# The outputs' products of a recurrence, with the two halves of the heads in two column groups of the array

## The chip, the core and the metric

The kernel runs on one core of one Trainium2 chip. The metric is the device time of one execution in microseconds (us); lower is better. Three runs of the kernel before gave a median of 1437.52 us (1435.84 to 1438.68).

## What is computed

Three stages follow each other: a recurrence over 768 tokens for 4 x 8 heads, a mixture of eight experts with two experts for each token, and a dense feed-forward layer. Only the first matters for the change:

```python
state = np.zeros((B, H, D, D))                       # B, H, S, D = 4, 8, 768, 40
for t in range(S):
    y[:, :, t] = np.einsum('bhd,bhde->bhe', rt, state)
    Sa = np.einsum('bhde,bhe->bhd', state, at)
    state = state * wt[:, :, None, :] - np.einsum('bhd,bhe->bhde', Sa, bt) + np.einsum('bhd,bhe->bhde', vt, kt)
...
x = y.transpose(0, 2, 1, 3).reshape(B * S, H * D)    # 3072 tokens x 320, goes to the experts
```

## The kernel before, in words

**The recurrence by chunks.** The tokens are cut into 24 chunks of 32. The 32 heads form two sets of 16, and each chunk is worked through once for each set, so there are 48 steps (`chain`, L604). A set's 16 heads are two halves `sg` of 8. What belongs to a chunk and not to the state (decays, products within the chunk, a triangular solve) is made ahead of the steps by three generators, `prepare`, `solve` and `apply`, whose instructions are dealt out between the parts of a step by `pump` at due times counted in steps.

**One step.** TensorE's order in step g is: the new states (`s_mm`, L559, tile `cu`); the transposes of the states (`tr`, L576, tile `ct`); the vectors u of the next step (`u_mm`, L546, tile `cu`); the outputs of the step before (`y_mm`, L522, tile `Y`); the products of r with v (`rv_mm`, L591, tile `ct`). Between them `fill` puts the work of the generators and of the routing. VectorE multiplies the new states by their decay (L564) and masks the products with v into the tile `RR` (L602); `tr` of the next step uses the buffers of `ct` that L602 frees.

**The outputs.** `y_mm` makes 16 products in each step, one for each head: weights `RR` of 128 rows x 32 columns (32 tokens), a moving operand `KB` of 128 rows x 40. In the trace each product is two instructions, as all of these f32 products are, so a step has 32 on L522. The four steps of two chunks fill the 128 partitions of two tiles `Y0` and `Y1` (one for each half), 32 partitions for each step: step c writes partitions 32 (c mod 4) onward of both. All 16 products of a step thus use one column group of the array, at `tile_position=(0, 32 (c % 4))`. `u_mm`, `s_mm` and `rv_mm` have a loop over `sg` inside the loop over heads, and the two halves go to different column groups (96 and 32 in `u_mm`, 0 and 64 in `s_mm` and `rv_mm`). After the fourth step ScalarE copies the two tiles to SBUF and GpSimd multiplies them by the decays `EN` of the same 128 tokens (VectorE does both from step 33 on, L532). The rows are then stored for the experts (L1687).

**The decays EN.** `turns` (L294) makes a chunk's decays with tokens on partitions: the 64 rows of chunk i go to rows 64 (i mod 2) onward of a tile `EN` that two chunks share (L317). `load_et` (L257) moves a chunk's 64 rows from `EN` to the two halves of a tile `ET` with two DMAs on SyncE's queue (SP), and GpSimd multiplies them with `a` (L268).

**Queues.** TensorE, ScalarE, VectorE and GpSimd run in the order in which the program is written. All loads and stores of the steps are issued by SP, whose order is left to the framework's scheduler (L1705 names the four others alone). For each chunk it issues, among others: `ET` (L262, two DMAs), `v` (L500, twice), `r` (L511 twice, L505), `w` and `k`, `b` (L201), the store of the chunk's products for the solve (L288), the load of `KB` (L495), the store `knd` of k and b turned (L308), the solved factors `Tbd` (L385, four) and `a` (L254).

**The order of tokens.** `ORDER` (L780) lists, for each tile of 128 tokens, which tokens lie on its partitions. The routing noise is laid out by it on the host, and the result is stored by it in runs of 32 rows (L1646). Tile 2 (c // 4) + sg holds the half `sg`.

Of the kernel before, what the change touches and what calls it, by code (L numbers as in the profile page):

```python
# [11 lines left out]
F32 = mybir.dt.float32  # L12
# [8 lines left out]
B, H, S, D = 4, 8, 768, 40  # L21
# [5 lines left out]
NG = NP * NC  # L27
# [37 lines left out]
class Rec:  # L65


    def __init__(self, ctx, nc, tc, ins, emit_x, ident, share, late):
        self.share, self.late = share, late
        self.nc, self.tc, self.ins, self.emit_x = nc, tc, ins, emit_x  # L70
        P = lambda n, b, **k: ctx.enter_context(tc.tile_pool(name=n, bufs=b, **k))
        self.one = P("rone", 1)
        self.p2, self.px = P("r2", 2), P("rx", 3)
        self.pet = P("ret", 1)
        self.pen = P("ren", 6)
        self.ptm, self.pwe = P("rtm", 2), P("rwe", 14)
        self.pp, self.py = P("rpp", 2, space=PS), P("rpy", 1, space=PS)
        self.cu, self.ct = P("rcu", 2, space=PS), P("rct", 2, space=PS)
        self.pd = P("rd", 2, space=bass.MemoryType.DRAM)
        self.pkn = P("rkn", 16, space=bass.MemoryType.DRAM)  # L80
        self.ident = ident
        self.scaled, self.lscr, self.tscr, self.Ec = {}, {}, {}, {}
        self.at = {}
        self.KN, self.ZT, self.EN, self.WE = {}, {}, {}, {}
        self.Y = {}
        self.seq = range(NC)
        self.extra, self.later, self.fresh = [], [], 0

# [168 lines left out]
    def load_et(self, i):  # L257

        en, et = self.EN[i // 2], self.at[i][1]
        r = 64 * (i % 2)  # L260
        for ab in range(2):
            self.nc.sync.dma_start(out=et[64 * ab:64 * ab + 64], in_=en[r:r + 64, ab])  # L262

    def scale_a(self, i):
        self.ready = i + 1
# [28 lines left out]
    def turns(self, i):  # L294

        nc = self.nc
        pt4 = lambda: self.pp.tile([128, 512], F32, name="pp")
        half = lambda x: x.rearrange("p (h x) -> p h x", x=64)[:, :, 0:D]
        kn, kb, Ec = self.p2.tile([128, HH, D], F32, name="kn"), self.kbt(i), self.Ec.pop(i)
        flip = lambda out, x: nc.tensor.transpose(out, x, self.ident[0:RW, 0:RW])  # L300
        for sg in range(2):
            yield
            pt = pt4()
            for p in range(4):
                flip(pt[:, p * 128:p * 128 + RW], kb[0:RW, sg * 4 + p].rearrange("p b s c -> p (b s c)"))
            nc.scalar.copy(out=kn[:, sg * 8:sg * 8 + 8], in_=half(pt))
        self.KN[i] = self.pkn.tile([64, 2 * HH * D], F32, name="knd")
        (nc.scalar if i < OPT['dk'] else nc.sync).dma_start(out=self.KN[i].rearrange("r (c x) -> c r x", c=2), in_=kn.rearrange("p h d -> p (h d)"))  # L308
        if i % 2 == 0:
            self.EN[i // 2] = self.pen.tile([128, 2, PR, D], F32, name="EN")  # L310
        en, r0 = self.EN[i // 2], 64 * (i % 2)
        for sg in range(2):
            yield
            pt = pt4()
            for p in range(4):
                flip(pt[0:64, p * 128:p * 128 + RW], Ec[0:RW, sg * 4 + p, :])
            nc.scalar.copy(out=en[r0:r0 + 64, :, sg * 4:sg * 4 + 4, :].rearrange("t b p d -> t p b d"),  # L317
                           in_=half(pt[0:64]).rearrange("t (p b) d -> t p b d", b=2))
# [191 lines left out]
            for ab in range(2):  # L510
                nc.sync.dma_start(out=self.rbd[i % 2][64 * ab:64 * ab + D, ab].rearrange("p a b c -> p (a b c)"), in_=ins["r"][i, ab])  # L511

    def y_mm(self, g, sg):
        nc = self.nc
        c = g
        r0 = 32 * (c % 4)
        if c % 4 == 0:
            self.Y[sg] = self.py.tile([128, 8, D], F32, name=f"Y{sg}")
        y = self.Y[sg]
        for h in range(8):  # L520
            hh = sg * 8 + h
            nc.tensor.matmul(y[r0:r0 + 32, h, :], lhsT=self.RR[c % 4][:, hh, :],  # L522
                             rhs=self.KB[(c // 2) % 2][:, c % 2, 1, hh, :], start=True, stop=True,
                             tile_position=(0, r0))
        if c % 4 == 3:
            x = self.px.tile([128, 8, D], F32, name="X") if g < NG - 1 else self.last_x[sg]
            en = self.EN[c // 4]
            dve = g in OPT['yd'] or g >= OPT['yv']
            if not dve:
                nc.scalar.copy(out=x, in_=y)  # L530
                y = x
            (nc.vector if dve else nc.gpsimd).tensor_tensor(  # L532
                out=x.rearrange("t (p b) d -> t p b d", b=2), in0=y.rearrange("t (p b) d -> t p b d", b=2),
                in1=en[:, :, sg * 4:sg * 4 + 4].rearrange("t b p d -> t p b d"), op=ALU.mult)
            self.extra.append(self.emit_x(2 * (c // 4) + sg, x))
# [68 lines left out]
    def chain(self, g, fill):  # L604
        if g == 0:
            self.u_mm(0)
        if g < NG - 2:
            if OPT['va']:
                self.load_v(g + 2)
            if g % NP == 0 and OPT['rb'] == 0:  # L610
                self.load_rbd(g // NP + 1)
            if g % NP and OPT['ra'] == 1 and g + 1 < NG:
                self.load_r(g // NP + 1)
            if g % NP and OPT['kb'] == 1 and g > 1:
                self.load_kb(g // NP + 1)
            self.s_mm(g)
        fill()
        trs = []
        for sg in range(2):
            trs.append(self.tr(g, sg))  # L620
            fill()
        if g + 1 < NG:
            self.u_mm(g + 1)
        fill()
        for sg in range(2):
            if g:
                self.y_mm(g - 1, sg)
        if g + 2 < NG:
            if not OPT['va']:
                self.load_v(g + 2)  # L630
            if g % NP == 0 and OPT['ra'] == 0:
                self.load_r(g // NP + 1)
            if g % NP == 0 and OPT['rb'] == 1:
                self.load_rbd(g // NP + 1)
            if g % NP == 0 and g and OPT['kb'] == 0:
                self.load_kb(g // NP + 1)
        fill()
        self.rv_mm(g, trs)
        fill()
# [49 lines left out]
    def run(self):  # L689
        nc = self.nc  # L690
        INF = 1e9
        self.consts_a()
        self.consts_b()
        gens = [self.prepare(), self.solve(), self.apply()]
        pos = []

        def pump(tau):
            while min(pos) <= tau:
                i = pos.index(min(pos))

                while i and self.wants[i]():
                    i = self.wants[i]() - 1
                pos[i] = next(gens[i], INF)

        tag = [None]

        def side(k=0):


            if self.extra and (not self.later or not self.fresh and (k == 5 if self.hurry else k % 3)):  # L710
                if next(self.extra[0], INF) is INF:
                    self.extra.pop(0)
                return
            if tag[0] == "act" and k:
                return
            two = True
            self.fresh = max(0, self.fresh - 1)
            while self.later:
                tag[0] = next(self.later[0], INF)
                if tag[0] is INF:  # L720
                    self.later.pop(0)
                elif tag[0] == "two" and two:
                    two = False
                else:
                    break

        self.made = self.ready = self.solved = 0
        self.wants = [None, lambda: 0, lambda: 0]
        self.begin()
        pos += [next(g) for g in gens]  # L730
        pump(-9)
        pump(-1)
        pump(OPT["t0"])
        f = np.cumsum((0,) + OPT["f"]) / sum(OPT["f"])
        for c in range(NG):
            self.hurry = c >= OPT["hurry"]
            slot = iter(enumerate(f[1:]))

            def fill():
                k, x = next(slot)  # L740
                pump(self.tau(c + x))
                side(k)

            self.chain(c, fill)
            if c == 2:
                self.tables()
            if c == NG - 2:
                self.late()
        for sg in range(2):
            self.y_mm(NG - 1, sg)  # L750
        while self.extra or self.later:
            side(1)
            side(0)
# [24 lines left out]


ORDER = np.arange(N).reshape(2, 2, NT // 2, 2, 32).transpose(2, 1, 3, 0, 4).reshape(NT, 128)  # L780


def xrow(n):
# [953 lines left out]
```

## Time and profile before

| | |
|---|---|
| median of three runs | 1437.52 us |
| the profiled execution | 1428.78 us |
| its span, first to last instruction | 1427.0 us |
| mean granted TensorE clock | 0.914 |
| TensorE matmuls, weight loads | 1193.8 us (84%), 1139.8 us (80%) |
| VectorE, ScalarE, GpSimd | 862.7 us (60%), 665.6 us (47%), 625.5 us (44%) |
| matmuls on L522 | 1536, from 135.1 to 600.0 us |

Shares are of the span. A matmul's duration runs from its start to its modelled end, and neighbours overlap, so what a block of matmuls costs is read from the start of one block to the start of the next. "Idle before" is the time in which the engine did nothing ahead of an instruction, with the one that ended it.

### The profile page before, as it was taken

The page shows a single profiled execution, that of the slowest core. Times are in us where ns is not written, and L with a number is a line of the kernel's source. Part 1 is how long each engine was busy: PE and PEld are TensorE (multiplying, and loading weights), DVE is VectorE, ACT ScalarE, POOL GpSimd, SP SyncE. Part 2 cuts the span into 40 slices and gives each one's busy share as a digit, 9 for nine tenths or more (in the row PEclk, how much of TensorE's full clock was granted, in tenths as well). Part 3 has the DMA queues.
Part 4 walks back from the last instruction along what each step waited for, and adds up shares of the span by engine and source line. Part 5 has one row for each costly group of instructions (what it writes and reads, how often), then busy time and mean ns, then how long its engine had stood idle before and what let it go on. Part 6 is the DMA issues. An engine that isn't in the chain of part 4 may idle for free. (4 is left out here: it accounts for less than half of the span.)

```text
span 1427.0 us, 33994 instructions
## 1 busy us (share of the span) xinstructions
PE 1193.8 (84%) x13902; PEld 1139.8 (80%) x13902; DVE 862.7 (60%) x1570; ACT 665.6 (47%) x1419; POOL 625.5 (44%) x556
## 2 busy tenths in 40 slices
PE   3425778878787886786999999998898999999998
PEld 2325767767677775775999998998888999999998
DVE  8474838657593833272877876775336665556653
ACT  3423545545444433431443443443236666676664
POOL 5553735546271624162334533443045554454431
PEclk9557989989889988897999999999998999999999
DMA  6644667666755754424345545644245111110000
GB/s 152 156 134 127 163 159 187 173 164 178 174 128 119 133 95 89 132 86 133 106 125 173 161 147 168 214 133 155 77 138 132 28 35 32 28 47 10 15 15 20
DMA packets 147309, 165.64 MB, mean 116 GB/s; under 512 B 70295, under 2 KB 118423, under 8 KB 147127
## 3 DMA queue, kind: packets, MB, share of 16 engines
q1 hardware_dynamic: 136438, 140.85, 37.6%
q0 software_dynamic: 10688, 22.32, 5.9%
q8 instruction: 120, 1.97, 0.6%
q14 instruction: 63, 0.51, 0.1%
HBM read 116.06 MB, written 43.12 MB: 112 GB/s over the span
## 5 line engine op out<-in xcount | busy, mean ns | idle before, releaser
L1609 POOL TENSOR_TENSOR gl<-fh,gh 128x1024 fp32r<-128x1024 f32 x46 | 131.0, 2878 | 106.2 <-ACT gh L1625 102.8
L1251 PE MATMUL ph<-xh,w1h 128*128 128x256 f32 (+1 forms) x576 | 162.1, 294 | 8.3 <-ACTq L1403 5.2
L1251 PE MATMUL ph<-xl,w1h 128*128 128x256 f32 (+1 forms) x576 | 161.8, 294 | 0.1
L1577 PE MATMUL fps<-fxh,ih 128*128 128x256 f32 x576 | 157.7, 288 | 2.2 <-DVE fh L1579 2.2
L1577 PE MATMUL fps<-fxl,ih 128*128 128x256 f32 x576 | 155.0, 283 | 0.1
L1608 DVE TENSOR_TENSOR fh<-fh,fp 128x1024 f32<-128x1024 f32 x48 | 95.0, 2015 | 61.4 <-ACT fp L1607 61.4
L1271 PE MATMUL py<-w2h,hl 128*128 128x320 f32 x400 | 125.7, 314 | 6.2 <-DVE hl L1105 6.1
L1271 PE MATMUL py<-w2h,hh 128*128 128x320 f32 x400 | 129.3, 323 | 1.0 <-ACT y L1282 0.8
L1271 PE MATMUL py<-w2l,hh 128*128 128x320 f32 x400 | 125.2, 313 | 2.5 <-DVE w2l L1107 1.5
L1105 DVE SCALAR_TENSOR_TENSOR hl<-ph,hh 128x512 fp32r<-128x512 f32 (+1 forms) x104 | 69.0, 665 | 95.1 <-ACT hh L1103 85.6
L1251 PEld LDWEIGHTS ph<-xh,w1h 128*128 128x128 f32 x576 | 113.3, 197 | 9.1 <-issue 5.7
L1639 PE MATMUL fpy<-oh,gl 128*128 128x320 f32 x384 | 114.6, 310 | 0.0
L1639 PE MATMUL fpy<-oh,gh 128*128 128x320 f32 x384 | 114.3, 310 | 0.0
L1639 PE MATMUL fpy<-ol,gh 128*128 128x320 f32 x384 | 113.9, 308 | 0.0
L1251 PEld LDWEIGHTS ph<-xl,w1h 128*128 128x128 f32 x576 | 113.3, 197 | 0.5 <-DVE xl L1107 0.5
L1579 DVE COPY fh<-fps 128x512 f32<-128x512 f32 x96 | 64.8, 689 | 80.7 <-ACT fp L1578 75.7
L1251 PE MATMUL ph<-xh,w1l 128*128 128x256 f32 (+1 forms) x384 | 112.7, 293 | 0.0
L1577 PEld LDWEIGHTS fps<-fxh,ih 128*128 128x128 f32 x576 | 110.2, 191 | 2.5 <-DVE fh L1579 2.4
L1577 PEld LDWEIGHTS fps<-fxl,ih 128*128 128x128 f32 x576 | 110.2, 191 | 0.6 <-DVE fxl L1107 0.5
L1577 PE MATMUL fps<-fxh,il 128*128 128x256 f32 x384 | 108.5, 282 | 0.0
L1103 ACT ACTIVATE hh<-ph 128x512 fp32r<-128x512 f32 (+1 forms) x104 | 59.6, 580 | 90.6 <-PE ph L1251 82.7
L602 DVE TENSOR_TENSOR RR<-ct,mrv 64x256 f32<-64x256 f32 x96 | 40.6, 423 | 91.3 <-PE ct L591 77.7
(276 smaller groups left out, 3352.6 us busy)
## 6 DMA issues: line engine op xcount, KB each, us to landing
KB<-knd SPq DMA_DIRECT2D x24, 640.0 KB
share<-in_w_dram SPq DMA_DIRECT2D x8, 1280.0 KB
wa<-in_wa_dram SPq DMA_DIRECT2D x22, 422.9 KB
kb<-in_kb_dram SPq DMA_DIRECT2D x20, 416.0 KB
share<-in_w_dram SPq DMA_DIRECT2D x8, 1024.0 KB
knd<-kn SPq DMA_DIRECT2D x24, 320.0 KB
yb<-y SPq DMA_DIRECT2D x22, 320.0 KB
ST<-in_vn_dram SPq DMA_DIRECT2D x48, 128.0 KB
```

The lines of the kernel that those rows point to most:

```text
L602: nc.vector.tensor_tensor(out=ro, in0=rvv, in1=self.mrv[r, None, :].to_broadcast([64, 8, C]), op=ALU.mult)
L1103: nc.scalar.activation(out=hi, in_=src, func=AF.Relu if relu else AF.Copy)
L1105: nc.vector.scalar_tensor_tensor(out=lo, in0=src, scalar=0.0, in1=hi.bitcast(F32), op0=ALU.max, op1=ALU.subtract)
L1251: nc.tensor.matmul(ph[:, m % c], lhsT=a, rhs=b, start=(q == 0), stop=(q == len(ops) - 1))
L1271: nc.tensor.matmul(py, lhsT=a[:, m, ts], rhs=b[:, m], start=(m == 0 and q == 0), stop=(m == FC - 1 and q == 2))
L1577: nc.tensor.matmul(ph[:, i], lhsT=a, rhs=b, start=(q == 0), stop=(q == len(ops) - 1))
L1579: nc.vector.tensor_copy(h[:, 2 * m2:2 * m2 + 2], ph)
L1608: mul = lambda s: nc.vector.tensor_tensor(out=h[:, s], in0=h[:, s], in1=p[:, s], op=ALU.mult)
L1609: low = lambda s: (nc.vector if last and s.start % 8 else nc.gpsimd).tensor_tensor(out=gl[:, s], in0=h[:, s], in1=gh[:, s].bitcast(F32), o ...
L1639: nc.tensor.matmul(py, lhsT=a[:, m, ts], rhs=w[:, m], start=(q == 0), stop=(q == len(ops) - 1))
```

## The change

The loop over `sg` moves inside the loop over heads, and the second half's tile `Y1` is filled from partition 64 on, modulo 128. The two products that follow each other then write partitions 64 apart. For the rows of `Y1` to meet their decays, `EN` holds the second half's columns with the two chunks' rows exchanged; a chunk's 64 rows of `EN` are no longer contiguous in partitions over both halves, and `load_et` issues four DMAs of half the bytes. The tokens of the odd tiles are turned by 64 in `ORDER`.

```diff
     def load_et(self, i):
         en, et = self.EN[i // 2], self.at[i][1]
-        r = 64 * (i % 2)
         for ab in range(2):
-            self.nc.sync.dma_start(out=et[64 * ab:64 * ab + 64], in_=en[r:r + 64, ab])
+            for sg in range(2):
+                r, p = self.enrow(i, sg), slice(4 * sg, 4 * sg + 4)
+                self.nc.sync.dma_start(out=et[64 * ab:64 * ab + 64, p], in_=en[r:r + 64, ab, p])
+
+    def enrow(self, i, sg):
+        return 64 * ((i + sg) % 2)
...
-        en, r0 = self.EN[i // 2], 64 * (i % 2)
+        en = self.EN[i // 2]
         for sg in range(2):
+            r0 = self.enrow(i, sg)
...
-    def y_mm(self, g, sg):
+    def y_mm(self, g):
         nc = self.nc
         c = g
-        r0 = 32 * (c % 4)
         if c % 4 == 0:
-            self.Y[sg] = self.py.tile([128, 8, D], F32, name=f"Y{sg}")
-        y = self.Y[sg]
+            self.Y = [self.py.tile([128, 8, D], F32, name=f"Y{sg}") for sg in range(2)]
         for h in range(8):
-            hh = sg * 8 + h
-            nc.tensor.matmul(y[r0:r0 + 32, h, :], lhsT=self.RR[c % 4][:, hh, :],
-                             rhs=self.KB[(c // 2) % 2][:, c % 2, 1, hh, :], start=True, stop=True,
-                             tile_position=(0, r0))
-        if c % 4 == 3:
+            for sg in range(2):
+                hh = sg * 8 + h
+                r0 = (32 * (c % 4) + 64 * sg) % 128
+                nc.tensor.matmul(self.Y[sg][r0:r0 + 32, h, :], lhsT=self.RR[c % 4][:, hh, :],
+                                 rhs=self.KB[(c // 2) % 2][:, c % 2, 1, hh, :], start=True, stop=True,
+                                 tile_position=(0, r0))
+        for sg in range(2 if c % 4 == 3 else 0):
+            y = self.Y[sg]
...
 ORDER = np.arange(N).reshape(2, 2, NT // 2, 2, 32).transpose(2, 1, 3, 0, 4).reshape(NT, 128)
+ORDER[1::2] = np.roll(ORDER[1::2], 64, axis=1)
```

The two places that call `y_mm` now call it once for a step instead of once for each half.

## Rows read from the trace of the kernel before

**Rows 1.** Busy time of each engine by stretch; then TensorE's clock, DMA share, GB/s

```profile
135.00:465.00 330.00, 261.97 (x5433) 238.12 (x5427) 214.52 (x312) 164.31 (x483) 165.11 (x110) 0.89 0.64 159
465.00:600.00 135.00, 104.22 (x1935) 93.99 (x1932) 60.17 (x136) 51.59 (x160) 49.69 (x74) 0.85 0.53 104
600.00:800.00 200.00, 173.50 (x1216) 169.06 (x1214) 128.91 (x351) 72.88 (x160) 80.70 (x93) 0.93 0.44 127
800.00:1427.00 627.00, 600.53 (x4487) 594.56 (x4486) 371.98 (x668) 331.07 (x512) 270.07 (x190) 0.98 0.29 86
```

**Rows 2.** TensorE's waits, 135 to 465 us: total us, times, longest

```profile
PE cu L559 <- DMA KB<-knd: 26.3, 9, 5.9
PE ct L576 <- DVE RR L602: 25.9, 13, 5.9
PE cu L546 <- DMA ST<-in_vn_dram: 10.6, 6, 4.6
```

**Rows 3.** TensorE's waits for L602, 465 to 600 us

```profile
PE ct L576 <- DVE RR L602: 4.8, 2, 2.7
```

**Rows 4.** VectorE's waits for TensorE's L591, 465 to 600 us

```profile
DVE RR L602 <- PE ct L591: 36.5, 12, 10.6
```

**Rows 5.** SP's queue in order of time: start, us, line, DMA

```profile
293.87 1.15 SPq L262 DMA_DIRECT2D ET<-EN  x2
...
298.85 0.64 SPq L495 DMA_DIRECT2D KB<-knd  x1
299.58 0.55 SPq L308 DMA_DIRECT2D knd<-kn  x1
...
310.25 0.39 SPq L254 DMA_DIRECT2D AT<-in_at_dram  x1
314.46 1.15 SPq L262 DMA_DIRECT2D ET<-EN  x2
```

**Rows 6.** SP's waits, 135 to 465 us

```profile
SPq L262 <- DMA knd<-kn: 26.2, 10, 3.8
...
SPq L495 <- PE pp L300: 9.9, 2, 5.2
```

**Rows 7.** Groups of TensorE's matmuls by line and shape, 135 to 600 us

```profile
L522 PE MATMUL Y<-KB,RR 128*32 128x40 f32 x1534 | 73.4, 214 | 3.3 <-issue 3.3
...
L546 PE MATMUL cu<-ST,Zt 128*32 128x40 f32 x1460 | 43.6, 218 | 27.3 <-DVE ST L564 13.2 <-DMA ST<-in_vn_dram 10.6 <-issue 2.5
```

**Rows 8.** TensorE in order of time, a step at 294 us

```profile
294.28 0.77 PE L546 MATMUL cu<-ST,Zt 128*32 128x40 f32 x32 [0.43 <-DMA ST<-in_vn_dram]
294.84 1.31 PE L522 MATMUL Y<-KB,RR 128*32 128x40 f32 x32
296.09 0.57 PE L300 MATMUL pp<-ident,kb 104*128 104x104 f32 x4
```

**Rows 9.** TensorE in order of time, a step at 421 us

```profile
420.93 1.28 PE L546 MATMUL cu<-ST,Zt 128*32 128x40 f32 x32
422.00 2.08 PE L522 MATMUL Y<-KB,RR 128*32 128x40 f32 x32
424.02 0.58 PE L300 MATMUL pp<-ident,kb 104*128 104x104 f32 x4
```

**Rows 10.** The stretches of rows 8 and rows 9, columns as in rows 1

```profile
294.00:296.40 2.40, 2.12 (x67) 2.10 (x68) 0.00 (x0) 2.10 (x7) 0.00 (x0) 1.00 0.43 94
420.30:423.60 3.30, 3.30 (x60) 3.15 (x60) 3.23 (x3) 2.48 (x8) 3.22 (x2) 0.50 0.20 35
```

**Rows 11.** VectorE in order of time, at 330 us

```profile
330.03 3.51 DVE L227 TENSOR_TENSOR_SCAN R<-wa,d1b 104x529 f32<-104x529 f32 x1
333.57 0.88 DVE L602 TENSOR_TENSOR RR<-ct,mrv 64x256 f32<-64x256 f32 x2
```

**Rows 12.** TensorE in order of time, what follows rows 11

```profile
334.04 0.66 PE L576 MATMUL ct<-ident,ST 128*128 128x128 f32 x4 [1.93 <-DVE RR L602]
```

**Rows 13.** All DMA issues of L262: ns min/median/max, first and last start

```profile
L262 SPq DMA_DIRECT2D ET<-EN x44: 224/584/1653, 35.9 to 466.4; - x44
```

More of the change, by code (lines that the diff above doesn't have):

```diff
@@ L84, in __init__ @@
         self.KN, self.ZT, self.EN, self.WE = {}, {}, {}, {}
-        self.Y = {}
         self.seq = range(NC)
@@ L624, in chain @@
         fill()
-        for sg in range(2):
-            if g:
-                self.y_mm(g - 1, sg)
+        if g:
+            self.y_mm(g - 1)
         if g + 2 < NG:
@@ L748, in run @@
                 self.late()
-        for sg in range(2):
-            self.y_mm(NG - 1, sg)
+        self.y_mm(NG - 1)
         while self.extra or self.later:
```

## The prediction

> **What bounds the kernel now.** I read the stretches first, then each stretch's waits, then the queues in order of time. The change touches the 48 steps, 135 to 600 us; what follows is TensorE's (173.50 busy of 200 us, then 600.53 of 627) [rows 1] and, as data, stays the same, so I take an earlier or later end of the steps to move the end of the kernel by as much.
>
> The steps fall into two parts. Up to about 465 us there are 32 steps, and TensorE is busy 262 of 330 us [rows 1]. What it waits for there is not its own: the load of `KB` 26.3 us, VectorE's L602 25.9 us, the load of `v` 10.6 us [rows 2]. From 465 us on there are 16 steps and 104 us of work in 135 us; the wait for L602 is down to 4.8 us [rows 3], and it is VectorE that waits for TensorE, 36.5 us in 12 of the 16 steps [rows 4]. So TensorE paces the second part and mostly not the first.
>
> The pace of the first part is seen on SP. The `ET` loads start at 293.87 and again at 314.46 us, 20.6 us apart, which is two steps [rows 5]. Before the second, SP does nothing from 310.64 us on, and the wait is for the store `knd` [rows 5, 6]: issued at 299.58 us, it has landed 14.9 us later. From the first `ET` to that store SP issues one DMA behind another for 5.7 us [rows 5]. 5.7 + 14.9 = 20.6 us: SP and the DMAs alone make a loop as long as two steps. It is not always the last: in two chunks SP waited for TensorE ahead of `KB`, 9.9 us [rows 6].
>
> **The part that gains.** L522 is 1534 of the records of 135 to 600 us [rows 7]. What a step's 32 cost is read from block to block: at 294 us L546 takes 0.56 us from its start to that of L522, L522 1.25 us to the start of what follows [rows 8]. At 421 us it is 1.07 against 2.02 us [rows 9]. The granted clock is 1.00 in the first stretch and 0.50 in the second, the two levels 2.4 and 1.2 GHz [rows 10]. L546 has the same 32 instructions with weights of 128 x 32 and a moving operand of 128 x 40 [rows 7]; it differs in that neighbours write to different column groups, as L522's will. I take its price: 1.25 - 0.56 = 0.69 us at the full clock, of which I keep 0.6 us for a step, since a block that another shape follows pays for that change before and after, and about 0.95 us at the half clock. Below that, a gain of zero is possible if the alternation is not what makes L546 fast; above, 0.69 us is the most.
>
> A rule of the Trainium skill speaks against it: by the page "TensorE: Matmul & The Clock Gate", section "Part 3: Packing small matmuls — row/col tiling", a weight load overlaps running matmuls only where the row groups differ; here all use all 128 rows. By that L522 would stay at 1.25 us; the row of L546 [rows 8], all 128 rows too, does not agree, and I go by it.
>
> In the second part 12 steps, in which VectorE waits [rows 4], give 12 x 0.6 = 7.2 us; some half clock there and a few steps late in the first part in which nothing but TensorE is late add about 1.8 us. That is **-9.0 us**. In the rest of the first part I give the saving nothing: where a load or L602 is late, TensorE only waits longer. At 330 us, for one, VectorE is still in a 3.51 us scan when the products are long done, L602 follows at 333.57 us, and `tr` has waited 1.93 us [rows 11, 12]. If every step passed its saving on, it would be 48 x 0.6 = 29 us; the waits of [rows 2] exclude most of that.
>
> **The part that costs.** `load_et` issues two more DMAs for a chunk. The 44 issues took 584 ns in the median, 224 at the least [rows 13]; a pair at 314.46 us took 1.15 us [rows 5]. Half the bytes in the same 64 rows: no row shows the half size, so between 2 x 0.22 = 0.45 and 1.2 us; I take 1.2, since the issue keeps SP for the rows and not for the bytes as far as a neighbour in [rows 5] tells (`KB`, by its shape with eight times the bytes of one `ET` load, takes 0.64 us). They stand at the start of the 5.7 us ahead of the next `KB` and `knd`, behind the wait for the old `knd`, and queued behind them on SP are `v`, `r`, `w`, `KB` and `knd` themselves; for `KB` and `v` TensorE waits [rows 2]. The first part holds 330 / 20.6 = 16 chunks. In ten the wait for `knd` stands right ahead of `ET` [rows 6]; take off two in which SP waits for TensorE later anyway, and 8 x 1.2 = **+9.6 us** remain. Bounds: nothing, if SP's idle time takes the issues up; 12 x 1.2 = 14.4 us if the loop holds in all but the late chunks.
>
> **What costs nothing.** The same products, copies and multiplications run. The copies of Y0 used to start after half of the 1.25 us block; now after all of a block half as long, so no later. `turns` writes other partitions of `EN` with the same copies. The order of tokens changes no size. The halved rows of `ET` add 128 packets to a chunk; the DMA share in the first part is 0.64 [rows 1], and GpSimd's L268, which waits for `ET`, feeds work two chunks later; were that cover gone, it would be part of the 1.2 us bound. Two more DMAs may also shift which earlier DMA a later one of SP's waits is for; the one that SP stands at is ahead of the first `ET` [rows 5, 6] and stays there, so I put the rest at nothing, with the 14.4 us as its upper bound too.
>
> **Sum.** -9.0 + 9.6 = +0.6 us on the profiled 1428.78 us, 1429.4. The median of the runs lies 8.7 us above that execution, so 1438 us as a median: no change that a measurement of this kernel can tell (about 0.2%, 2.9 us).
>
> **The rivals.**
> *SP has room* (chance 0.27). The issues of half the size are short, or the loads have slack before TensorE needs them, and the loop's length does not matter. For it: in the steps at 330 us VectorE and not a load is last [rows 11, 12]. Against it: the 26.3 and 10.6 us of [rows 2]. Then -9 us stand alone: 1428.5 us.
> *SP's loop decides: slower* (0.19). The place is between the landing of one `knd` and the issue of the next; the price 1.2 us for a chunk; from 7.5 chunks on it eats the gain of 9 us, and from ten on the kernel is slower beyond doubt. With 12 chunks, 14.4 us, and 7 us gained because the last steps find another wait (their 4.8 us for L602 grow [rows 3]): +7.4, 1445 us. For it: the exact 5.7 + 14.9 of [rows 5].
> *The products do not overlap* (0.06). The change then does not do what it says: L522 stays at 1.25 us a block, and only the DMAs show: +9.6, 1447 us. Against it is L546 [rows 8]; this is the skill page's rule at work.
> *TensorE paces more than the waits show* (0.06): half of the first part's steps pass on 0.6 us too, and SP has room: -9 - 9.6, 1419 us.
>
> **How the numbers follow.** My forecast has 0.42 and a range of its own of 1433 to 1443: a couple of chunks or steps more or less. Of it 0.26 falls within 0.2%, 0.07 below, 0.09 above. SP's room gives 0.25 to faster and 0.02 to the same, the deciding loop 0.17 to slower and 0.02 to the same, the last two 0.06 each to slower and faster. Faster 0.38, same 0.30, slower 0.32. The range from 1427 to 1448 holds all but the last rival and the outer halves of the first two, within 2 in 10.
>
> **What the profile of the changed kernel would show.** The block of L522 at 0.55 to 0.65 us at the full clock; unchanged, the first step is wrong. Four `ET` issues in about 2.3 us, and `ET` to `knd` near 6.9 us; if it is 5.7 to 6.2, the price was too high. `ET` to `ET` near 21.8 us and TensorE's waits for `KB` and `v` clearly above 26.3 and 10.6 us: the loop holds. If two chunks still take 20.6 us, SP had room. The stretch from the end of the `ET` loads to the end of L522 some 8 us shorter. The forecast is wrong if the store `knd` is no longer what SP waits for, or if the scheduler orders SP's queue anew.

## The result, and the profile after

The changed kernel takes 1450.45 us in the median of six runs (1443.52 to 1455.35), the kernel before 1436.19 us (1430.49 to 1438.68) beside it: a ratio of 1.0111 [1.0077, 1.0144], 14 us slower. The forecast was no change, 1438 us, with a range up to 1448. The profiled execution took 1453.06 us with a span of 1451.3 us, against 1428.78 and 1427.0 us.

First the products themselves. TensorE in order of time in two steps of the changed kernel (start and duration in us), and below the two stretches with the granted clock third from the end:

```profile
305.81 0.80 PE L553 MATMUL cu<-ST,Zt 128*32 128x40 f32 x32 [0.31 <-DMA ST<-in_vn_dram]
306.42 0.76 PE L528 MATMUL Y<-KB,RR 128*32 128x40 f32 x32
307.11 0.58 PE L304 MATMUL pp<-ident,kb 104*128 104x104 f32 x4
...
392.12 1.33 PE L528 MATMUL Y<-KB,RR 128*32 128x40 f32 x32
393.38 0.96 PE L304 MATMUL pp<-ident,kb 104*128 104x104 f32 x4
```

```profile
391.50:393.50 2.00, 2.00 (x60) 1.91 (x55) 0.00 (x0) 0.91 (x3) 0.00 (x0) 0.50 0.36 85
306.40:307.10 0.70, 0.70 (x44) 0.66 (x37) 0.00 (x0) 0.52 (x3) 0.00 (x0) 1.00 0.37 92
```

From the start of the block of outputs (L528) to the start of what follows it is 0.69 us at a granted clock of 1.00 (2.4 GHz) and 1.26 us at 0.50 (1.2 GHz), against 1.25 and 2.02 us [rows 8, 9]. The two column groups do what they were to do: 0.56 us less per step at the full clock and 0.76 us at half of it.

The time is lost elsewhere. Busy time by stretch in the changed kernel (columns as in rows 1), and TensorE's waits from 135 to 465 us:

```profile
135.00:465.00 330.00, 239.94 (x5212) 216.70 (x5210) 212.35 (x309) 155.98 (x460) 160.90 (x107) 0.85 0.60 152
465.00:600.00 135.00, 90.23 (x1815) 81.08 (x1814) 57.65 (x131) 49.58 (x150) 48.19 (x73) 0.82 0.55 98
```

```profile
PE cu L566 <- DMA KB<-knd: 39.8, 10, 7.1
PE ct L583 <- DVE RR L609: 31.9, 9, 6.1
PE pp L407 <- DMA Tbd<-tscr: 6.1, 3, 2.3
PE cu L553 <- DMA ST<-in_vn_dram: 5.4, 4, 2.5
```

TensorE gets through fewer matmuls in the same 330 us (5212 against 5433 [rows 1]; of its busy time, 239.94 against 261.97 us, a part is only the shorter products), and waits 39.8 us for `KB` where it waited 26.3 us [rows 2]. Who makes `KB` late is seen on SP's queue, two steps in order of time, with SP's longest wait and all of its `ET` issues (ns min/median/max):

```profile
305.24 2.43 SPq L262 DMA_DIRECT2D ET<-EN  x4
...
311.26 0.64 SPq L500 DMA_DIRECT2D KB<-knd  x1
312.05 0.58 SPq L312 DMA_DIRECT2D knd<-kn  x1
312.69 1.92 SPq L505 DMA_DIRECT2D ST<-in_vn_dram  x1
314.66 0.34 SPq L510 DMA_DIRECT2D RR<-in_rt_dram  x1
315.04 7.78 SPq L390 DMA_DIRECT2D Tbd<-tscr  x4
322.93 1.51 SPq L253 DMA_DIRECT2D AT<-in_at_dram  x1
326.99 2.42 SPq L262 DMA_DIRECT2D ET<-EN  x4
```

```profile
SPq L262 <- DMA knd<-kn: 35.2, 12, 5.3
```

```profile
L262 SPq DMA_DIRECT2D ET<-EN x88: 461/595/1600, 35.1 to 489.2; - x88
```

From the first `ET` to `knd` it is 6.8 us (5.7 before [rows 5]), from there to the next `ET` 14.9 us as before, together 21.75 us for two steps in place of 20.6. With half the bytes an `ET` issue still takes 595 ns in the median (584 before [rows 13]). How this adds up over the 24 chunks is read from the first and the last issue of `knd`, of which each chunk has one. The kernel before, then the changed one:

```profile
L308 SPq DMA_DIRECT2D knd<-kn x24: 524/553/1451, 34.5 to 445.2; - x24
```

```profile
L312 SPq DMA_DIRECT2D knd<-kn x24: 528/554/714, 34.4 to 464.7; - x24
```

410.7 us became 430.3 us: +19.6 us before the 24th `knd`. Behind it, over the last 18 steps, the two are equal although the products are shorter: the last products start at 600.0 and at 619.2 us, 154.8 and 154.5 us after the last `knd`. The remaining 5 us of the spans' difference come later: ahead of the group L1257 (L1251 before) TensorE was idle for 13.7 us against 8.3 us, in a stage that the change does not touch.

### The profile page after: what moved, and what is told of

Its sections match the earlier page's. It is cut to its first block, busy times and chain, and to the rows that moved or that the text cites. A ratio compares the mean times of both kernels' runs of the same rounds, so it can differ in the third digit from the quotient of the medians.

```text
span 1451.3 us, 34061 instructions
## 1 busy us (share of the span) xinstructions
PE 1173.7 (81%) x13902; PEld 1118.2 (77%) x13902; DVE 859.9 (59%) x1570; ACT 665.1 (46%) x1419; POOL 621.4 (43%) x556
## 5 line engine op out<-in xcount | busy, mean ns | idle before, releaser
L1257 PE MATMUL ph<-xh,w1h 128*128 128x256 f32 (+1 forms) x576 | 162.2, 294 | 13.7 <-issue 10.0
L1257 PE MATMUL ph<-xl,w1h 128*128 128x256 f32 (+1 forms) x576 | 161.3, 293 | 0.5 <-DVE xl L1113 0.4
L1257 PEld LDWEIGHTS ph<-xh,w1h 128*128 128x128 f32 x576 | 113.3, 197 | 14.5 <-issue 10.5
L1257 PEld LDWEIGHTS ph<-xl,w1h 128*128 128x128 f32 x576 | 113.2, 197 | 0.9 <-DVE xl L1113 0.9
L1257 PE MATMUL ph<-xh,w1l 128*128 128x256 f32 (+1 forms) x384 | 112.0, 292 | 0.0
L583 PE MATMUL ct<-ident,ST 128*128 128x128 f32 x384 | 71.9, 322 | 44.3 <-DVE RR L609 43.1
## 6 DMA issues: line engine op xcount, KB each, us to landing
wa<-in_wa_dram SPq DMA_DIRECT2D x22, 422.9 KB
```

What stands on the lines that cost most here:

```text
L583: nc.tensor.transpose(tr[:, p, :], ST[:, sg * 4 + p].rearrange("p b x -> p (b x)"), self.ident)
L1257: nc.tensor.matmul(ph[:, m % c], lhsT=a, rhs=b, start=(q == 0), stop=(q == len(ops) - 1))
```

## The experiments

Each group of kernels was timed beside the kernel before on one chip. The time is the difference of the two medians; the ratio, with its 95% interval, is that of the runs of both and can differ from it by some us (the changed kernel again: +24.1 us, but 0.0139 x 1409 = 19.6 us). "knd" is the time from the first to the last issue of `knd` in the one execution that was profiled, as read above, against the 410.7 us of the kernel before; two executions of one kernel agree within 1 us (430.3 and 431.1, 410.7 and 409.7, 406.6 and 406.2). All results first, then the groups; "four loads" and "groups" are the two halves of the change.

| kernel | time against before, us | ratio | knd, us |
|---|---|---|---|
| four loads of ET alone | +20.5 | 1.0142 [1.0104, 1.0180] | 427.9 |
| three loads alone | +10.9 | 1.0070 [1.0047, 1.0094] | 419.7 |
| groups alone | -0.7 | 0.9988 [0.9961, 1.0014] | 407.7 |
| the changed kernel again | +24.1 | 1.0139 [1.0099, 1.0179] | 431.1 |
| before, again (one execution) | | | 409.7 |
| changed, two loads on ACT | +10.5 | 1.0080 [1.0051, 1.0109] | 424.6 |
| before, one load on ACT | -2.1 | 0.9994 [0.9962, 1.0026] | 405.5 |
| groups, one load on ACT | -2.9 | 0.9981 [0.9951, 1.0012] | 412.6 |
| before, knd on ACT | +18.2 | 1.0150 [1.0113, 1.0187] | 432.5 |
| changed, knd on ACT | +50.1 | 1.0368 [1.0333, 1.0404] | 460.0 |
| groups, knd on ACT | +12.6 | 1.0102 [1.0065, 1.0139] | 435.1 |
| before, products twice | +10.4 | 1.0085 [1.0050, 1.0119] | 409.9 |
| before, kb and wa on POOL | -5.2 | 0.9958 [0.9934, 0.9981] | 406.6 |
| changed, kb and wa on POOL | -2.5 | 0.9986 [0.9963, 1.0008] | 409.2 |
| spare loads behind knd | +14.4 | 1.0122 [1.0092, 1.0152] | 420.4 |
| spare loads behind ET | +17.4 | 1.0130 [1.0103, 1.0156] | 429.2 |
| groups, kb and wa on POOL | -14.0 | 0.9917 [0.9888, 0.9946] | 401.7 |
| before, kb and wa on POOL, again | -7.6 | 0.9948 [0.9925, 0.9971] | 406.2 |

**The two halves of the change, each alone.** The first kernel has the products as before and each `ET` load cut in two; the second has the column groups and two `ET` loads, `EN` and the token order as before; the copy of the second tile exchanges its halves instead, as two instructions of 64 rows each (where VectorE does the work, its multiplication). These few instructions are added work that the changed kernel does not have.

```diff
-            self.nc.sync.dma_start(out=et[64 * ab:64 * ab + 64], in_=en[r:r + 64, ab])
+            for sg in range(2):
+                p = slice(4 * sg, 4 * sg + 4)
+                self.nc.sync.dma_start(out=et[64 * ab:64 * ab + 64, p], in_=en[r:r + 64, ab, p])
```

```diff
+            rows = [(slice(0, 128), slice(0, 128))] if not sg else [(slice(0, 64), slice(64, 128)), (slice(64, 128), slice(0, 64))]
...
-                nc.scalar.copy(out=x, in_=y)
+                for o, s in rows:
+                    nc.scalar.copy(out=x[o], in_=y[s])
```

> The kernel before with ET loaded in four DMAs of half the bytes, and nothing else of the change (products of the outputs in one column group, EN and the order of tokens as before). If SP's loop is the cause: slower by 16 to 24 us (at least what the changed kernel loses, 14 us, as the shorter products no longer give anything back), ET to ET near 21.3 us for two steps. If the column groups are the cause (TensorE less busy, its clock granted less often): within 3 us of before, clock near 0.914. If it is the exchanged rows of EN or the turned tokens: within 3 us of before.

> The two halves in two column groups as in the changed kernel, but ET in two DMAs, EN and the order of tokens as before; the second half's rows are put back in place when Y is copied out (six more copies of ScalarE and a few more products of VectorE in all). If SP's loop is the cause: faster than before by 2 to 9 us, ET to ET near 19.8 to 20.6 us. If the column groups are the cause: slower by about 14 us, clock near 0.90. If EN or the tokens: faster or the same.

> The kernel before with ET loaded in three DMAs (one whole, two halves). If SP's loop is the cause and each issue has its price: about half of what four loads cost, slower by 8 to 12 us. If the column groups, EN or the tokens are the cause: within 3 us of before.

> The changed kernel itself, on the chip of the three others, so that the four cases (one or two column groups, two or four loads) stand side by side. By every theory 1.1% slower than before, 1446 to 1455 us. If SP's loop is the cause it is a little faster than the kernel with four loads and one column group, by the 2 to 9 us that the shorter products give.

The loads alone cost all of it (+20.5 us), the groups alone nothing that shows, and one added load costs half of what two do. The changed kernel and the four loads alone stand within their intervals of each other, so the groups win nothing that shows on top of the loads either, and there without the added copies. Both misses of the 2 to 9 us expected of the groups are taken up further below. TensorE's granted clock is too little changed to be the loads' cost: 0.914 in the median of the runs of the four loads alone, 0.918 in the kernel before beside them, and 0.004 x 1409 us are 6 us at most. TensorE's waits for `KB` in the four loads alone are those of the changed kernel:

```profile
PE cu L561 <- DMA KB<-knd: 39.7, 11, 6.4
```

**Two loads, or one, on another queue.** In each kernel the named loads are issued by ACT:

```diff
-                self.nc.sync.dma_start(out=et[64 * ab:64 * ab + 64, p], in_=en[r:r + 64, ab, p])
+                (self.nc.scalar if sg else self.nc.sync).dma_start(out=et[64 * ab:64 * ab + 64, p], in_=en[r:r + 64, ab, p])
```

> The kernel before once more, unchanged, for its trace beside those of the other runs of this chip. Its profiled execution should lie near 1409 us, the median that the kernel before had beside the first four experiments. Of its stretches: if the loss of the four loads lies in SP's loop alone, its 13 periods of two steps between the ninth and the 22nd landing of knd take about 257 us, as in the two column groups alone (257.0), against 271 to 275 with four loads; if it lies elsewhere, the periods are as long as with four loads and the tail is shorter.

> The changed kernel with its four loads of ET kept, two of them (the second half of heads) issued by ACT's queue and two by SP's as before. Bytes, packets and the number of transfers are those of the changed kernel. If SP's time for the two added issues is the loss, it is won back: 0 to 5 us against the kernel before (ratio 1.000 to 1.004), the periods of two steps back at 19.8 us from 21.2. If it is the added transfers themselves (packets, the transfers' landing), +20 to +24 us stay (1.014 to 1.017). If ACT, held by the two issues and by their wait for a free ET, takes SP's place, something in between or worse, with ACT's copies of EN late.

> The kernel before with one of its two loads of ET issued by ACT's queue: one issue per chunk less on SP. If SP's loop still sets the pace at its present length, the line through three and four loads (+10.9 and +20.5 us for one and two more) goes on below: -8 to -11 us (ratio about 0.993), 19.1 us for a period of two steps instead of 19.8. If the loop is only just the bound and another engine's pace lies close under it, 0 to -4 us. If ACT is the one held, slower, by 2 to 10 us.

> The two column groups alone (as in the second experiment), with one of the two loads of ET issued by ACT's queue. If the column groups bought nothing because SP's loop set the pace, then with SP relieved they pay: 3 to 9 us faster than the same relief without the groups. If TensorE's saved 0.6 us a step is absorbed by other waits as well (DVE's RR, the chain of the steps), the two are within 2 us of each other.

The kernel before once more took 1425 us in its one execution and not the 1409 us expected; its trace has the stall told of at the end, and its `knd` time is that of before. With two loads on ACT half of the loss comes back (+10.5 us): in between, as the third case had it, but the wait that shows is SP's. Its waits from 135 to 465 us in the changed kernel with two loads on ACT:

```profile
SPq L390 <- DMA ET<-EN: 24.9, 10, 12.2
SPq L510 <- DMA ET<-EN: 14.9, 2, 7.6
```

SP now stands at `Tbd` and `RR` until an `ET` transfer has landed, though neither reads `ET`; with all of `ET` on SP (the kernel before, the changed one, the four loads alone) SP has no wait for `ET`. One `ET` issue less on SP, with and without the groups, brings 2 to 3 us, inside the intervals and not the 8 to 11 of a line that goes on. This does not show how close SP's loop is to the next bound, since here, too, SP gained waits for `ET` (25.0 us at `Tbd` and 22.2 us at `AT` without the groups).

**knd on ACT's queue.** From the ninth chunk on, the store that SP waits for is issued by ACT (`nc.scalar if i >= 8`), in the kernel before, the changed one, and the groups alone.

> The kernel before with the store of knd issued by ACT's queue from the ninth chunk on. In the kernel before, SP waits at the first load of ET until knd has landed (some 14 us after its issue), and the next knd is issued some 6 us after that landing: 14 + 6 are the 20 us of a period of two steps. If this ring of knd's landing and the issues behind it is the pace, taking knd out of SP's queue opens it: periods of 17 to 19 us and 10 to 35 us less in all, or as much as the next bound allows. If the pace is the transfers' own rate or the chain of the steps, and SP only follows, the periods stay at 19.8 us and the time within 4 us of before. If ACT's own wait for a free place for knd's transfer takes the place of SP's, the periods stay or grow, with ACT late at TRs.

> The changed kernel, four loads of ET on SP and all, with knd issued by ACT's queue from the ninth chunk on. If the four loads cost what they do because they lie between one landing of knd and the issue of the next, most of their price goes with the ring: within 5 us of the same edit in the kernel before. If an added issue costs its SP time wherever SP is, or the added transfers cost their own time, the changed kernel stays 15 to 22 us behind the same edit in the kernel before.

> The two column groups alone (two loads of ET on SP, rows put back by the copy), with knd issued by ACT's queue from the ninth chunk on. If the column groups bought nothing because SP's ring set the pace, they pay here: 4 to 9 us less than the same edit in the kernel before. If their 0.6 us a step is lost in the chain of the steps too, the two are within 3 us.

All three got slower, which only the last case of the first expectation had. The changed kernel lost 50 us, 32 us more than the same move cost the kernel before, beyond both cases expected; the groups came out 5.6 us below it, as expected if they pay, but the two intervals overlap. The wait was not opened but moved; SP's waits of the kernel before with `knd` on ACT, 135 to 465 us:

```profile
SPq L500 <- DMA knd<-kn: 44.5, 4, 14.8
SPq L201 <- DMA knd<-kn: 30.6, 4, 10.9
SPq L1687 <- DMA knd<-kn: 22.8, 2, 11.5
SPq L505 <- DMA knd<-kn: 22.4, 2, 11.5
```

Loads that have no use for `knd` wait for it, up to 14.8 us at a time. In the changed kernel's queue, shown above, the first `ET` is the eighth DMA behind `knd` (`ST`, `RR`, four `Tbd`, `AT`, then `ET`; the kernel before has the same order), and `ET` does not read `knd` either. My guess, not shown, is that DMAs share a few completion counters in turn; the runs show which DMA waits for which, not the counters.

**The products twice.** `for h in (*range(8), *range(8))` in the kernel before: 55 us more work for TensorE.

> The kernel before with every block of the outputs' products done twice over, with the same result: 1.15 us more of TensorE per step at full clock (32 more instructions of 36 ns), 55 us over 48 steps. If TensorE paces only the last 16 steps, as the prediction had it, the time grows by 1.15 us in about 12 of them and by a little in the rest: 12 to 20 us. If TensorE has room nearly everywhere, 0 to 6 us. If TensorE paces the first part too, and the column groups' gain was lost for another reason, 40 to 55 us.

A block of 64 took 2.39 us, from its start to the next:

```profile
294.58 2.46 PE L522 MATMUL Y<-KB,RR 128*32 128x40 f32 x64
296.97 0.58 PE L300 MATMUL pp<-ident,kb 104*128 104x104 f32 x4
```

The 24 chunks took 409.9 us, as without the extra work: up to the last `knd` TensorE has room for 1.15 us a step more. What the time grew by lies behind it: 10.4 us by the medians, 12 us by the ratio (7 to 17 us by its interval), at the lower end of what was expected if TensorE paces the last steps alone. The 18 steps from the last `knd` to the last products, with the products twice and then in the four loads alone, a trace without the stall told of at the end as well (columns as in rows 1):

```profile
443.90:600.50 156.60, 133.73 (x2776) 125.10 (x2775) 62.49 (x142) 61.06 (x187) 50.34 (x77) 0.92 0.61 114
```

```profile
462.20:597.10 134.90, 111.00 (x2168) 103.03 (x2168) 61.91 (x140) 60.22 (x186) 49.16 (x74) 0.92 0.64 119
```

In the six traces with one column group and without the stall this stretch takes 133 to 137 us, so the doubled products add some 20 us here, about all of their 18 x 1.15 = 20.7 us: added work does arrive in these steps. Why the time grew by less is open, since there is no trace of the kernel before from this group of runs.

**kb and wa on POOL's queue, and spare loads.** Two kernels take two SP issues per chunk away that have nothing to do with `ET`, from the ninth chunk on; two others, the kernel before each, add two loads that nobody reads (64 rows of 640 B from `EN`), in two places of SP's queue.

```diff
-        self.nc.sync.dma_start(out=out[0:rows], in_=self.ins[x][i, 0:rows])
+        (self.nc.gpsimd if i >= 8 else self.nc.sync).dma_start(out=out[0:rows], in_=self.ins[x][i, 0:rows])
```

```diff
+    def spares(self, i):
+        if i >= 8:
+            for k in range(2):
+                self.nc.sync.dma_start(out=self.spare[k], in_=self.EN[i // 2 - 1][64 * (i % 2):64 * (i % 2) + 64, k, 0:4])
```

> The kernel before with the loads of kb and wa issued by POOL's queue from the ninth chunk on: two SP issues per period of two steps less (0.52 and 0.31 us), the same transfers. If SP's issue time behind knd's landing is the pace, 0.8 us a period and 10 to 14 us in all are won (periods of 19.0 us). If the transfers' order in the queue, or the lane that a transfer shares with the one eight before it, is what counts, the periods move otherwise: 19.5 us or more, the time within 5 us of before or above it.

> The changed kernel with the same two loads issued by POOL's queue from the ninth chunk on: SP has two issues more for ET and two fewer for kb and wa, 1.2 against 0.8 us a period. If SP's issue time is the loss, 10 to 14 of the changed kernel's 20 us come back (ratio to before 1.004 to 1.008). If the added transfers themselves cost, or the issue's place, 18 to 22 us stay (1.012 to 1.016).

> The kernel before with two added transfers per chunk from the ninth chunk on (64 rows of 640 B from EN into a tile that nobody reads), issued right behind knd, in the 14 us in which SP otherwise waits for knd to land. If what counts is SP's time between a landing of knd and its next issue, they cost less than the same two issued behind ET: 0 to 8 us. If every added transfer costs alike wherever it is issued (its bytes, its packets), both kernels lose the same, 14 to 20 us.

> The same two added transfers per chunk, issued right behind the loads of ET, where the changed kernel has its own two. If the loss is SP's time between knd's landing and its next issue, it is that of the four loads of ET for 16 chunks of 24: 13 to 18 us, periods of 20.9 us. If it came from POOL's or ACT's wait for ET in four parts, nothing is read from the added tiles here, and the time is that of before within 4 us.

Loads without a reader cost what the four loads of `ET` cost: +17.4 us for 16 chunks against +20.5 us for 24. So it is not that GpSimd waits for an `ET` in four parts. Behind `knd`, in the 14 us in which SP otherwise waits, they cost 14.4 us where 0 to 8 were expected: my idea that only the time between a landing of `knd` and the next `knd` is paid for was wrong. The place may still count for something: the intervals of the two times overlap, but the `knd` times, 420.4 and 429.2 us, lie 9 us apart. An added DMA behind `knd` makes an earlier one the eighth: SP there waited for `knd` at the `Tbd` loads, 45.7 us in 10 waits.

And with `kb` and `wa` off SP the changed kernel, four `ET` issues and all, loses nothing against the kernel before: more came back than either case had. So the added transfers by themselves cost little there (0.9986, against 0.9958 for the kernel before with the same move). The move gives the kernel before 5.2 us, half of the least expected if SP's issue time sets the pace. TensorE's first waits from 135 to 465 us, in the kernel before with this move, then in the changed kernel with it:

```profile
PE ct L576 <- DVE RR L602: 39.5, 17, 5.4
PE cu L546 <- DMA ST<-in_vn_dram: 8.9, 3, 3.7
PE cu L559 <- DMA KB<-knd: 5.8, 1, 5.8
```

```profile
PE ct L583 <- DVE RR L609: 40.4, 13, 7.3
PE pp L407 <- DMA Tbd<-tscr: 10.0, 2, 6.1
PE pp L407 <- DMA RR<-in_rt_dram: 9.2, 2, 4.6
PE cu L566 <- DMA KB<-knd: 5.8, 1, 5.8
```

The wait for `KB`, 26.3 us before and 39.8 us after the change, is 5.8 us in both, and VectorE's L602 (L609) is the longest: I take it for the next bound, close under SP's, since the kernel before gains so little. Two effects of the move are not separated: SP issues less, and some 840 KB a chunk (`kb` 416 KB, `wa` 422.9 KB by the profile's DMA issues) no longer stand ahead of `KB` in SP's queue.

**The groups with SP relieved.**

> The two column groups alone (two loads of ET, rows put back by the copy) with the loads of kb and wa issued by POOL's queue from the ninth chunk on. The same move of kb and wa gave the kernel before 5 us (ratio 0.996). If the column groups bought nothing because SP was the pace, they pay now: ratio 0.989 to 0.993. If the block of the outputs' products is not on the path in most steps even so, the ratio is that of the move alone, 0.994 to 0.998.

> The kernel before with the loads of kb and wa on POOL's queue once more. The same move together with the two column groups gave a ratio of 0.9917 [0.9888, 0.9946] on another chip than the move alone, 0.9958 [0.9934, 0.9981], and chips differ in a stall of VectorE of 18 us near 556 us. If the groups are what made the difference, the move alone stays at 0.994 to 0.998 here; if it was the chip, it comes to 0.990 to 0.993.

The groups with the move come to 0.9917, the move alone to 0.9958 and 0.9948, each on another chip and each where it was expected if the groups pay. The points lie 4 to 6 us apart and the intervals just overlap. That groups pay once SP is relieved is likely, and not shown. The version with both has the lowest ratio of all kernels here.

## Why the prediction was wrong

**The gain per step** was right: 0.6 us a step was given at the full clock and 0.95 us at half of it, 0.56 and 0.76 us were measured. The rule of the Trainium skill that spoke against it ("TensorE: Matmul & The Clock Gate", "Part 3: Packing small matmuls — row/col tiling": a weight load overlaps running matmuls only where the row groups differ) would have left the block at 1.25 us. The trace does not agree: all 128 rows are used throughout, and L528 went to 0.69 us.

**The gain that reaches the end** (-9.0 us) failed. "In the second part 12 steps, in which VectorE waits, give 12 x 0.6 = 7.2 us" took VectorE's wait for TensorE as proof that what TensorE saves arrives at the end. The groups alone measure -0.7 us [-5.5, +2.0] (the ratio's interval times 1409 us). In the changed kernel the last 135 us of the steps, with VectorE's waits and TensorE's:

```profile
484.20:619.20 135.00, 93.76 (x1897) 84.06 (x1895) 59.93 (x135) 51.13 (x159) 50.38 (x76) 0.84 0.58 117
```

```profile
DVE RR L609 <- PE ct L598: 32.7, 9, 9.3
DVE ST L571 <- remote: 21.5, 2, 20.4
```

```profile
PE cu L553 <- DVE ST L571: 16.8, 2, 16.6
PE ct L583 <- DVE RR L609: 10.9, 2, 8.0
```

TensorE is busy for 93.76 us where it was 104.22 in the same length [rows 1]: the saving is there, and TensorE stands idle for it. VectorE's wait for the products with v shrank from 36.5 us [rows 4] to 32.7 us; TensorE's wait for L609 grew from 4.8 us [rows 3] to 10.9 us, which the prediction named only in its rival with 7 us gained, and the stall told of at the end, the two rows of ST, was some 3 us longer here.

Two more things stand in the record. In pairs of traces that differ in the groups alone, the 18 steps behind the last `knd` went from 152.8 to 146.7 us (one load on ACT), from 151.8 to 145.6 us (`kb` and `wa` on POOL, on two chips) and from 137.1 to 138.7 us (`knd` on ACT), one execution each. So in two of three pairs a gain of about the size forecast did arrive, and in the first of them the 24 chunks took 7.1 us longer instead. And TensorE's granted clock moved with the length of these blocks: beside the kernel before at 0.918, the groups alone had 0.9105 in the median of 12 runs, and the products twice had 0.9315 in the median of 8, beside 0.916. By these clocks 0.0075 x 1409 = 11 us of TensorE's time at the full clock went with the groups, an estimate; a block of L528 takes 1.26 us at half the clock and 0.69 us at full. That, and the waits above, can take up a saving of 48 x 0.56 = 27 us. No run separates them, so what holds each of these last steps stays open.

**Nothing gained in the first part** was right in the main: there even 1.15 us a step more cost nothing, at a granted clock of 0.94 from 135 us to the last `knd` where the kernel before had 0.88.

**The price of the issues** was right (1.2 us for two; `ET` x4 in 2.43 us; 6.8 us from `ET` to `knd`, 6.9 foretold; 21.75 us for two steps, 21.8 foretold; `KB` waits grown as foretold; the wait for `v`, foretold to grow as well, fell to 5.4 us).

**The number of chunks that pay it** failed: "take off two in which SP waits for TensorE later anyway, and 8 x 1.2 = +9.6 us remain", with 14.4 us as the bound. Four loads alone cost 20.5 us, over twice that, and above the bound: the price of 17 chunks and not of 8. The count went by those chunks in which SP's wait for `knd` stood right ahead of `ET` [rows 6], ten of 16; but 17.2 us of the 20.5 come between the first and the last `knd` (427.9 against 410.7 us), 23 intervals of 0.75 us, and the third load costs what the fourth does (10.9 and 9.6 us). SP's wait for `knd` can also stand at another DMA: in the changed kernel L390 waited for it as well, 9.0 us in two waits, so chunks without a wait at `ET` can pay too; which chunks paid was not read one by one. And the two spare loads behind `knd` show that the place is no refuge. The rival *SP's loop decides: slower* had the mechanism, and 1445 us because of the same count and of 7 us gained. Both errors pointed the same way, a gain too large and a cost too small, so nothing of them cancelled.

## What to carry to other kernels

When a change saves one engine's time and adds DMAs to a queue that issues in order, price the queue first: see whether one round of its issues and its longest wait is as long as the loop, and if so charge the added issues in every round and not only where the wait stands right ahead of them (here 0.75 us a round in the mean, of 1.2 us issued), whoever reads them. That an engine is waited for does not mean that a saving on it arrives: here doubled products cost some 20 us in the last 18 steps, while halved ones left TensorE idle and at a lower clock. Doubling a block tells what more of it costs, not what less of it gives. Here, cutting a transfer in two halved its bytes but not its issue, and moving two unrelated loads to another queue gave back all that the cut took.

## What was unexpected

**DMAs waited for others that they have no data from.** `ET` for `knd` in the kernel before, `Tbd` and `RR` up to 12.2 us for `ET` on ACT's queue, `ST`, `RR`, `xd` and the loads of L201 up to 14.8 us for `knd` on ACT's. Moving one DMA to a second queue thus made it a wait of the first.

**A stall of 18 us that came with the group of runs, not with the kernel.** VectorE's ST instruction near 570 us waited for something that the profile calls "remote", in the kernel before and, the same, in one of the variants (`kb` and `wa` on POOL, the second time):

```profile
574.80 1.01 DVE L564 TENSOR_TENSOR ST<-cu,WE 40x320 f32<-40x320 f32 x2 [18.18 <-remote]
```

```profile
568.41 1.01 DVE L564 TENSOR_TENSOR ST<-cu,WE 40x320 f32<-40x320 f32 x2 [18.11 <-remote]
```

The first run of that same variant has no such wait. Where the traces of a group of runs have it, the kernel before took 1431 to 1436 us in the median, elsewhere 1409 to 1417 us. Times here are therefore compared only within a group. Beside it GpSimd issued a series of 16 indirect transfers, 551.89 to 571.85 us in the kernel before. Such a series also stands in traces without the stall (with the products twice from 553.52 us on), so it is not enough by itself; what ties the two together, and why in some groups alone, was not tried.
